# Hash attention and a gelu feed-forward on one core: the order of the first loads and hashes, and the mark that lets GpSimd's weight sums go

## The chip, the cores and the metric

The kernel runs on one core of a Trainium2 chip. A core has a matrix engine (TensorE, "PE" in the profile; "PEld" is its loading of weights), a vector engine (VectorE, DVE), a scalar engine (ScalarE, ACT), a general engine (GpSimd, POOL) and an engine that issues transfers (SyncE, SP). Transfers are carried out by 16 DMA engines; here they are issued from the queues of SP and ACT. The metric is the device time of one execution in microseconds. Before the change it is 857.73 us, the median of three runs from 857.51 to 859.04.

## The reference

The reference is an attention in which a query sees only the keys of its own hash bucket, followed by a feed-forward block. Cut to what matters:

```python
# q, k, v: (4, 8, 768, 64) f32; proj: (64, 6); w_in: (512, 2048); w_out: (2048, 512)
q_bits = (einsum('bhsd,dk->bhsk', q, proj) > 0)
k_bits = (einsum('bhsd,dk->bhsk', k, proj) > 0)
mask = bucket(q_bits)[:, :, :, None] == bucket(k_bits)[:, :, None, :]
scores = where(mask, q @ k.T / sqrt(64), -1e9)
attn = softmax(scores)
x = (attn @ v).transpose(0, 2, 1, 3).reshape(3072, 512)
h = x @ w_in
g = h / (1 + exp(-1.702 * h))
out = g @ w_out
```

## The kernel before

The attention takes two heads at a time: 16 pairs, each with 768 queries in two halves (c = 0, 1) of 384 columns, and 768 keys in six tiles of 128. For each tile of keys `scores` (line 426) puts four products into one PSUM tile: two of bf16 hash features (`kf`, `qf`), which push the entries of other buckets far down, and two of the f32 operands (`kT`, `qT`). ACT takes the exponential into `es`; POOL and DVE add up the denominators (`add_low`, `add_high`); `values` multiplies with v; `total`, `invert` and `norm` divide by the sums.

For pairs 1 to 15 k and q come in already in blocks that DVE turns (`turn`), and their hash bits are made two pairs ahead (`hashed`, `featured`; the features then go through small transfers on SP). The first pair has no such lead and goes through `first_pair` (line 345). It issues, each half on SP and ACT, the loads of k, of the projections `pj`, and of q, in this order. PE runs four matmuls on a tile of zeros (`idle`, cleared by DVE at line 76) that nobody reads; `hash_weights` (line 123) makes the hash weights `pf_k`, `pf_q` (and the wide `pf0`) on DVE from `pj` in ten small instructions. `turned` transposes one half of k or q with PE against the identity, and a copy takes it out of PSUM: DVE for both halves of k, ACT for both halves of q. `bits` multiplies a half with the hash weights and DVE makes the features from it (line 377). `measure` lets ACT square k or q and add up (the `junk` rows; a guard against sizes that are too large). The call order is k half 0, k half 1, q half 0, q half 1, then the hashes of k half 0, q half 0, k half 1; the hash of q half 1 is called `rest` and follows the first three score tiles. The PSUM tiles of this stage come from one pool of three banks (`sps`, tag "s"), which the score tiles use afterwards; another pool, `mps` (tag "m"), has one bank that the pair's later hashes and the second half of the values use.

While the attention runs, w_in is read in chunks of 512 KB (`raw`, line 161) and converted by DVE in small steps (`convert`), one chunk for each pair from pair 2 on; `begin(n)` (line 517) issues the load and `step` the work. `behind(x)` (line 316) is a helper that lets DVE clear a few words of a tile that a load will overwrite, so that the load has to wait for this place in DVE's order. It stands ahead of two loads of the attention, pair 1's v and pair 2's q (pairs are counted from 0).

The feed-forward block follows. Both of its products are done by a scheme with seven block products in place of eight, which needs sums of blocks of the operands. In the second product, h w_out, there are 21 such steps (three blocks of tokens times the seven outer products, in the order `OUTER` = 1, 2, 6, 7, 5, 3, 4), and each step is itself seven products of 128x256 (`product_of_halves`, line 1066), in the order 1, 2, 3, 6, 7, 5, 4. A step needs four sums of its right operand, made by DVE in the step before (`g_sums`: t1, t2, d12, t4; line 222 makes t1, 224 t2, 223 d12 and 225 t4). The fourth product reads t2, the fifth d12, the sixth t1, the seventh t4. It also needs four sums of its left operand, the weights (`inner_sums`), of which the third product reads the last; these are made once, for the first block of tokens, by POOL. A copy of one element by POOL, the `mark` (line 1234), stands ahead of POOL's sums in steps 2, 3, 5 and 6, and makes POOL wait for the tile that it reads: in step n, the first quarter of the result of step n-1, `ms[OUTER[n-1]]`, which DVE writes early in step n-1. So the sums stand in step n's part of the program, but POOL makes them for step n+1 while step n-1 or n runs. Steps are counted from 0; step 0 starts at 593.82 us, and each takes about 12.1 us.

Four engines (PE, DVE, ACT, POOL) execute the order that the program writes; SP's transfers are put in order by a scheduler that takes their waits into account. The conversion of w_out and a second path for large inputs are not touched.

Of the kernel before, what the change touches and what calls it, by code (L numbers as in the profile page):

```python
# [8 lines left out]
F32 = mybir.dt.float32  # L9
BF16 = mybir.dt.bfloat16  # L10
# [9 lines left out]
P = 128  # L20
# [18 lines left out]
def kernel(  # L39
# [17 lines left out]
    nc = tc.nc  # L57

    loader = [nc.sync]
    B, H, S, D = q.shape  # L60
    NB = proj.shape[1]
# [6 lines left out]
    HS = HT * P  # L68
# [3 lines left out]
    fixed.enter_context(tc.manual_schedule(engines=ORDERED))  # L72
    const = ctx.enter_context(tc.tile_pool(name="const", bufs=1))

    idle = const.tile([P, 512], BF16, name="idle")
    nc.vector.memset(idle, 0.0)
    ident = const.tile([P, P], F32, name="ident")
    make_identity(nc, ident)
    ones = const.tile([P, D], F32, name="ones")
    nc.vector.memset(ones, 1.0)  # L80

    later = []

    pj = const.tile([P, NB], F32, name="pj")

    def offsets(name, row):
        x = const.tile([P, 1], F32, name=name)
# [63 lines left out]
    for x in (0x3FFFFFFF, 0xFF800000):  # L153
        m = const.tile([P, 1], U32, name=f"mask_{x:x}")
        later.append((m, x))
        masks[x] = m.to_broadcast([P, CW])

    def convert(cv, dst, src, queue=None, psum=None):


        raw = cv.tile([P, CW, 2], U32, tag="raw", name="raw")
        (queue or loader[0]).dma_start(out=raw, in_=src)

        def of(x):
            return x if len(dst.shape) == 2 else x.rearrange("p (x r) -> p x r", r=dst.shape[2])

        lo, hi = raw[:, :, 0], raw[:, :, 1]
        bits = cv.tile([P, CW], U32, tag="bits", name="bits")
        if psum is None:
            part, size = dst.bitcast(U32), hi.bitcast(F32)  # L170
        else:
            part = psum.tile([P, CW], U32, tag="part", name="part")
            size = psum.tile([P, CW], F32, tag="size", name="size")
        yield


        if psum is None:
            nc.vector.scalar_tensor_tensor(part, hi, 3, masks[0x3FFFFFFF], op0=Alu.logical_shift_left, op1=Alu.bitwise_and)
        else:
            nc.vector.tensor_scalar(part, hi, 3, 0x3FFFFFFF, op0=Alu.logical_shift_left, op1=Alu.bitwise_and)  # L180
        yield
        nc.vector.scalar_tensor_tensor(bits, hi, 0xC0000000, part, op0=Alu.bitwise_and, op1=Alu.bitwise_or)
        yield

        if psum is None:
            nc.vector.tensor_tensor(part, bits, masks[0xFF800000], op=Alu.bitwise_and)
        else:
            nc.vector.tensor_scalar(part, bits, 0xFF800000, None, op0=Alu.bitwise_and)

        nc.scalar.activation(size, hi.bitcast(F32), Act.Square)  # L190
        part = part.bitcast(F32)
        yield
        nc.vector.scalar_tensor_tensor(part, lo, 2.0**-52, part, op0=Alu.mult, op1=Alu.mult)
        yield
        bits = bits.bitcast(F32)
        whole = bits if psum is not None else dst
        nc.vector.tensor_tensor(whole, bits if psum is not None else of(bits), part if psum is not None else of(part), op=Alu.add)
        yield

        nc.vector.scalar_tensor_tensor(dst, of(size), (1.125 * 2.0**-15) ** 2, of(whole) if psum is not None else whole,  # L200
                                       op0=Alu.is_ge, op1=Alu.mult)
# [3 lines left out]
    in_chunks = [(w_in_sb[:, kc, f : f + CW], wi[kc, :, f : f + CW])  # L205
                 for f0 in range(0, FF // 2, CW) for f in (f0, FF // 2 + f0) for kc in range(KC)]
# [79 lines left out]
    def attention(ff):  # L286
# [4 lines left out]
        with actx:  # L291
            ld = actx.enter_context(tc.tile_pool(name="ld", bufs=1))
            wk = actx.enter_context(tc.tile_pool(name="wk", bufs=2))
            cv = actx.enter_context(tc.tile_pool(name="cv", bufs=1))
            st = actx.enter_context(tc.tile_pool(name="st", bufs=2))
            aps = actx.enter_context(tc.tile_pool(name="aps", bufs=1, space=PSUM))
            mps = actx.enter_context(tc.tile_pool(name="mps", bufs=1, space=PSUM))
            early = actx.enter_context(ExitStack())
            ep = early.enter_context(tc.tile_pool(name="ep", bufs=1))
            sps = early.enter_context(tc.tile_pool(name="sps", bufs=GT, space=PSUM))  # L300
# [44 lines left out]
            def first_pair():  # L345


                b, hp = pairs[0]
                x = {}
                for i, (name, src) in enumerate((("k", k), ("q", q))):  # L350
                    raw = raws[0, name] = ld.tile([P, S // 32, 32], F32, tag=name, name=name)
                    x[name] = raw.rearrange("p s i -> p (s i)").rearrange("p (j t d) -> p j t d", j=2, d=D)
                    for j, queue in enumerate((nc.sync, nc.scalar)):
                        queue.dma_start(out=x[name][:, j], in_=src[b, 2 * hp + j].rearrange("(p t) d -> p t d", p=P))
                    if i == 0:
                        for j, queue in enumerate((nc.sync, nc.scalar)):
                            queue.dma_start(out=pj[D * j : D * (j + 1)], in_=proj)
                    xts[0, name] = wk.tile([P, S], F32, tag=f"{name}T", name=f"{name}T")

                nc.scalar.activation(const.tile([1, 1], F32, name="first"), ones[0:1, 0:1], Act.Exp)  # L360
                for _ in range(4):
                    nc.tensor.matmul(aps.tile([P, 512], F32, tag="av", name="warm"), idle[:, 0:P], idle, start=True, stop=True)
                hash_weights()

                def turned(name, c, move):
                    tp = sps.tile([P, 2, 512], F32, tag="s", name="tp")[:, 0, 0:HS]
                    for i in range(GT):
                        for j in range(2):
                            nc.tensor.matmul(tp[D * j : D * (j + 1), i * P : (i + 1) * P], x[name][:, j, c * GT + i, :], ident,
                                             start=True, stop=True)  # L370
                    move(xts[0, name][:, c * HS : (c + 1) * HS], tp)

                def bits(name, c):
                    cols = slice(c * HS, (c + 1) * HS)
                    h = sps.tile([P, 2, 512], F32, tag="s", name="hash0")[:, 0, 0:HS]
                    nc.tensor.matmul(h, pf0[name].rearrange("p j d -> p (j d)"), xts[0, name][:, cols], start=True, stop=True)  # L376
                    nc.vector.tensor_scalar(feats[0][name][:, cols], h, above0[name][:, 0:1], FEAT[name],
                                            op0=Alu.is_gt, op1=Alu.mult)

                measure(0, "k")  # L380
                turned("k", 0, nc.vector.tensor_copy)
                turned("k", 1, nc.vector.tensor_copy)
                turned("q", 0, nc.scalar.copy)
                turned("q", 1, nc.scalar.copy)
                measure(0, "q")
                bits("k", 0)
                bits("q", 0)
                bits("k", 1)
                return lambda: bits("q", 1)

# [121 lines left out]
            conv = {}  # L512
# [4 lines left out]

            def begin(n):
                if 0 <= n - 2 < len(in_chunks) - LATE:
                    conv[n] = convert(cv, *in_chunks[n - 2])  # L520
                    step(n)


# [40 lines left out]
            for n in range(1, last + 1):  # L564
# [44 lines left out]
                if n < last:  # L609
                    begin(n + 1)  # L610
# [87 lines left out]
    def feed_forward(tag, late=()):  # L698
# [8 lines left out]
        OUTER = (1, 2, 6, 7, 5, 3, 4)  # L707
        with ExitStack() as fctx:
# [324 lines left out]
            def g_quarters(n):  # L1033
                if n not in g_tiles:


                    g_tiles[n] = wholes[4:6] if n == 1 else [
                        (st2 if n % 2 else gp).tile([P, F4, TH], F32, tag=t, name=t + "ab"[n % 2]) for t in ("t1", "t2")]
                    g_tiles[n] = g_tiles[n] + [gp.tile([P, F4, TH], F32, tag="t4", name="t4g")]
                g = raw_g[n % 2]  # L1040
                x = [g[:, F4 * k : F4 * (k + 1), TH * j : TH * (j + 1)] for k in range(2) for j in range(2)]
                return x + g_tiles[n]
# [9 lines left out]
            def turned(c, i, j, q0, q1):  # L1052

                for q in range(q0, q1):
                    h, k = divmod(q, 2)
                    y = ys[j].rearrange("p b (d r) -> p r b d", r=4)[:, 2 * i + h, k * (TH // 32) : (k + 1) * (TH // 32), :]
                    nc.vector.transpose(y, c[:, q].rearrange("p (b t) -> p b t", t=32))  # L1057
# [79 lines left out]
            cv = cv_ctx.enter_context(tc.tile_pool(name=f"cv{tag}", bufs=1))  # L1137
# [31 lines left out]
            x = todo.pop(1, [])  # L1169
# [56 lines left out]
            ms, pending = {}, []  # L1226
            mark = st2.tile([1, 1], F32, name="mark")
            for n, (sb, o) in enumerate(steps_out):
# [2 lines left out]
                    fetch(n + 1)  # L1231

                if n in (2, 3, 5, 6):
                    nc.gpsimd.tensor_copy(mark, ms[OUTER[n - 1]][0:1, 0, 0:1])
                for f in {2: inner_sums(3), 3: inner_sums(4), 5: inner_sums(5) + inner_sums(6)[:2], 6: inner_sums(6)[2:]}.get(n, []):
                    f()
                later_sums = g_sums(n + 1)
                m = wholes[n % len(wholes)]
# [92 lines left out]
```

## Time and profile before

| what | value |
|---|---|
| median of three runs | 857.73 us (857.51 to 859.04) |
| the profiled execution | 858.67 us |
| its span on the core | 856.80 us |
| granted TensorE clock, mean | 0.998 |
| PE busy, 0 to 11 us | 9.23 us |
| PE busy, 11 to 600 us | 588.9 of 589 us |
| PE busy, 627 to 640 us | 12.75 of 13 us |
| PE busy, 840 to 856.8 us | 8.29 of 16.8 us |
| DVE busy, 600 to 627 us | 25.67 of 27 us |
| POOL busy, 600 to 627 us | 17.66 of 27 us |

Busy times are those of the profiled execution. The starts in the order of time are counted from the start of its span, and 1.87 us lie outside it. A row of the order of time may hold several instructions in a row (xN); its duration reaches from the start of the first to the end of the last. What stands in brackets at its end is the idle time of the engine just before it, and what ended it.

### The profile page before, as it was taken

The page shows a single profiled execution, that of the slowest core. Times are in us where ns is not written, and L with a number is a line of the kernel's source. Part 1 is how long each engine was busy: PE and PEld are TensorE (multiplying, and loading weights), DVE is VectorE, ACT ScalarE, POOL GpSimd, SP SyncE. Part 2 cuts the span into 40 slices and gives each one's busy share as a digit, 9 for nine tenths or more (in the row PEclk, how much of TensorE's full clock was granted, in tenths as well). Part 3 has the DMA queues.
Part 4 walks back from the last instruction along what each step waited for, and adds up shares of the span by engine and source line. Part 5 has one row for each costly group of instructions (what it writes and reads, how often), then busy time and mean ns, then how long its engine had stood idle before and what let it go on. Part 6 is the DMA issues. An engine that isn't in the chain of part 4 may idle for free.

```text
span 856.8 us, 13648 instructions
## 1 busy us (share of the span) xinstructions
PE 846.2 (99%) x5007; PEld 529.2 (62%) x5007; DVE 703.3 (82%) x1072; ACT 344.9 (40%) x549; POOL 353.4 (41%) x316
## 2 busy tenths in 40 slices
PE   9999999999999999999999999999999999999996
PEld 4444444444444444566666666545888888888885
DVE  4589999999999885788987788577998977797776
ACT  5866667777666654343444444433000000000000
POOL 4343333433433359996854476669725000000000
PEclk9999999999999999999999999999999999999999
DMA  5625755445563104436555546587745685467524
GB/s 131 101 47 107 113 89 85 85 86 99 115 97 71 47 26 150 144 134 233 194 204 217 221 153 234 202 278 257 275 151 190 192 254 197 155 191 245 197 99 101
DMA packets 160987, 132.11 MB, mean 154 GB/s; under 512 B 122608, under 2 KB 137616, under 8 KB 155536
## 3 DMA queue, kind: packets, MB, share of 16 engines
q1 hardware_dynamic: 152016, 106.63, 45.0%
q10 hardware_dynamic: 8896, 24.53, 8.3%
q8 instruction: 41, 0.67, 0.3%
q14 instruction: 34, 0.28, 0.1%
HBM read 79.69 MB, written 50.33 MB: 152 GB/s over the span
## 4 chain that ended last, share of the span: by engine, by line
PE 96%; DVE 2%; DMA 1%; ACT 0%; issue 0%; ACTq 0%; SPq 0%; DVEq 0%
PE product L1077 28%; PE product L751 22%; PE ps L435 18%; PE av L468 15%; PE small L819 6%; PE product L819 3%; PE dn L489 1%; PE hash L411 1%; DVE xT L1081 1%; DVE y L1057 1%; DMA pj<-in_proj_dram 1%; PE hash L376 0%; DVE v L1081 0%; DVE raw_g L223 0%; DVE t2a L224 0%
## 5 line engine op out<-in xcount | busy, mean ns | idle before, releaser
L436 ACT ACTIVATE e<-ps 128x768 f32<-128x768 f32 x192 | 151.2, 812 | 25.7 <-PE ps L435 23.1
L435 PE MATMUL ps<-qT,kT 64*128 64x384 f32 x768 | 155.1, 482 | 0.0
L443 POOL TENSOR_TENSOR acc<-e 128x768 f32<-128x768 f32 x32 | 51.8, 1617 | 193.8 <-ACT e L436 174.3
L468 PE MATMUL av<-e,v 128*32 128x385 f32 x1536 | 128.0, 487 | 0.0
L751 PE MATMUL product<-xT,w_in_sb 128*128 128x512 f32 x216 | 100.1, 593 | 0.1
L468 PEld LDWEIGHTS av<-e,v 128*32 128x32 f32 x1536 | 48.5, 109 | 76.2 <-issue 74.6
L435 PEld LDWEIGHTS ps<-qT,kT 64*128 64x128 f32 x768 | 68.0, 187 | 38.5 <-issue 38.4
L751 PE MATMUL product<-t_x,s_in 128*128 128x512 f32 x192 | 89.4, 592 | 0.0
L1090 ACT COPY u<-product 128x256 f32<-128x256 f32 x21 | 7.8, 372 | 172.2 <-PE product L1077 139.0
L751 PEld LDWEIGHTS product<-xT,w_in_sb 128*128 128x128 f32 x216 | 40.9, 190 | 36.5 <-issue 33.0
L435 PE MATMUL ps<-qf,kf 64*128 64x384 bf16 x384 | 62.9, 324 | 0.1
L444 POOL TENSOR_TENSOR acc<-acc,e 128x768 f32<-128x768 f32 x32 | 55.8, 1744 | 2.5
L751 PEld LDWEIGHTS product<-t_x,s_in 128*128 128x128 f32 x192 | 36.5, 190 | 29.7 <-issue 26.8
L449 DVE SCALAR_TENSOR_TENSOR acc<-e 128x768 f32<-128x768 f32 x32 | 47.7, 1490 | 5.1 <-ACT e L436 5.1
L767 DVE TENSOR_TENSOR u<-product,u 128x256 f32<-128x256 f32 (+1 forms) x60 | 28.4, 486 | 16.4 <-PE product L819 13.2
L435 PEld LDWEIGHTS <-kf 64*128 64x128 bf16 x384 | 18.9, 94 | 35.1 <-issue 6.2
L451 DVE TENSOR_TENSOR acc<-acc,e 128x768 f32<-128x768 f32 x32 | 34.3, 1072 | 3.3
L451 DVE TENSOR_TENSOR acc<-acc,acc 128x768 f32<-128x768 f32 x32 | 31.2, 974 | 6.3 <-POOL acc L444 3.2
L1077 PE MATMUL product<-raw_g,xT 128*128 128x256 f32 x152 | 35.1, 379 | 0.0
L222 POOL TENSOR_TENSOR u<-v,u 128x1024 f32<-128x1024 f32 (+1 forms) x11 | 23.9, 2168 | 21.9 <-ACT v L764 8.1
L767 DVE TENSOR_TENSOR v<-product,v 128x512 f32<-128x512 f32 x24 | 16.5, 689 | 19.4 <-PE product L751 19.4
L767 DVE TENSOR_TENSOR c<-small,c 128x256 f32<-128x256 f32 (+1 forms) x54 | 24.1, 460 | 8.8 <-PE small L819 8.6
(278 smaller groups left out, 1727.3 us busy)
## 6 DMA issues: line engine op xcount, KB each, us to landing
raw_g<-g_dram SPq DMA_DIRECT2D x22, 1024.0 KB
s_in<-g_dram SPq DMA_DIRECT2D x20, 1024.0 KB
g_dram<-c ACTq DMA_DIRECT2D x18, 512.0 KB
raw<-in_moe_w_out_dram ACTq DMA_DIRECT2D x16, 512.0 KB
raw<-in_moe_w_in_dram SPq DMA_DIRECT2D x15, 512.0 KB
v<-in_v_dram SPq DMA_DIRECT2D x32, 192.0 KB
k<-in_k_dram SPq DMA_DIRECT2D x60, 96.0 KB
q<-in_q_dram SPq DMA_DIRECT2D x60, 96.0 KB
```

The source lines that it names most:

```text
L222: return [lambda: eng.tensor_tensor(t1, b12, b11, op=Alu.subtract), lambda: eng.tensor_tensor(b12, b22, b12, op=Alu.subtract), lambda: eng ...
L435: nc.tensor.matmul(ps[:, j, 0:HS], a[hs, keys], m[hs, cols], start=not last, stop=last)
L436: nc.scalar.activation(es[c][:, kt, :, 0:HS], ps[:, :, 0:HS], Act.Exp, scale=1.0 / D**0.5)
L443: nc.gpsimd.tensor_tensor(acc, es[c][:, 0, :, 0:HS], es[c][:, 1, :, 0:HS], op=Alu.add)
L444: nc.gpsimd.tensor_tensor(acc, acc, es[c][:, 2, :, 0:HS], op=Alu.add)
L449: nc.vector.scalar_tensor_tensor(acc, e[0], T * TINY, e[1], op0=Alu.add, op1=Alu.add)
L451: nc.vector.tensor_tensor(acc, acc, x, op=Alu.add)
L468: nc.tensor.matmul(av[D * j + d : D * j + d + 32, :], vt[:, t, j, d : d + 32], es[c][:, t, j, :], start=(t == 0), stop=(t == T - 1))
L751: nc.tensor.matmul(ps, wq[LEFT[i]][:, kc, :], xq[RIGHT[i]][:, kc, :], start=(start and kc == 0), stop=(kc == K2 - 1), skip_group_check=not ...
L767: nc.vector.tensor_tensor(dst, x, y, op=Alu.add)
L819: nc.tensor.matmul(x, wq[LEFT[i]], xq[RIGHT[i]], start=start, stop=True, skip_group_check=True)
L1077: nc.tensor.matmul(ps, wq[LEFT[i]][:, c, :], gq[RIGHT[i]][:, c, :], start=(c == 0), stop=(c == F4 - 1))
```

## The change

In the first pair, the loads of `pj` go behind those of q on both queues. The tile of zeros and its memset go; the warm-up now reads a constant 1.0 that the program's setup has written before the kernel's own instructions, and there are five matmuls in place of four. The first half of k is copied out of PSUM by ACT in place of DVE. The transposes of the second half of q move behind the hashes of k half 0 and q half 0, and ahead of the hash of k half 1; the hashes of q take their PSUM tile from `mps`.

The first chunk of w_in is now loaded with `behind`: one column of its tile is cleared by DVE in `begin(2)`, at the end of pair 1. In SP's order, its load moves from the place behind the first pair's v to the place behind the feature transfers of pair 3.

In steps 2 and 3 of the second product the mark reads t2 of the same step (`g_quarters(n)[5]`), which DVE writes late in step n-1, in place of the result of step n-1. Steps 5 and 6 keep theirs.

```diff
-    idle = const.tile([P, 512], BF16, name="idle")
-    nc.vector.memset(idle, 0.0)
+    pj = const.tile([P, NB], F32, name="pj")
...
-    def convert(cv, dst, src, queue=None, psum=None):
+    def convert(cv, dst, src, queue=None, psum=None, behind=None):
         raw = cv.tile([P, CW, 2], U32, tag="raw", name="raw")
+        if behind is not None:
+            behind(raw[:, 0, 0:1])
         (queue or loader[0]).dma_start(out=raw, in_=src)
...
                     for j, queue in enumerate((nc.sync, nc.scalar)):
                         queue.dma_start(out=x[name][:, j], in_=src[b, 2 * hp + j].rearrange("(p t) d -> p t d", p=P))
-                    if i == 0:
-                        for j, queue in enumerate((nc.sync, nc.scalar)):
-                            queue.dma_start(out=pj[D * j : D * (j + 1)], in_=proj)
                     xts[0, name] = wk.tile([P, S], F32, tag=f"{name}T", name=f"{name}T")
+                for j, queue in enumerate((nc.sync, nc.scalar)):
+                    queue.dma_start(out=pj[D * j : D * (j + 1)], in_=proj)
...
-                for _ in range(4):
-                    nc.tensor.matmul(aps.tile([P, 512], F32, tag="av", name="warm"), idle[:, 0:P], idle, start=True, stop=True)
+                for _ in range(5):
+                    one = [nc.const_aps.tensor(1.0, [P, x], BF16) for x in (P, 512)]
+                    nc.tensor.matmul(aps.tile([P, 512], F32, tag="av", name="warm"), *one, start=True, stop=True)
...
-                    h = sps.tile([P, 2, 512], F32, tag="s", name="hash0")[:, 0, 0:HS]
+                    if name == "q":
+                        h = mps.tile([P, HS], F32, tag="m", name="hash0")
+                    else:
+                        h = sps.tile([P, 2, 512], F32, tag="s", name="hash0")[:, 0, 0:HS]
...
-                turned("k", 0, nc.vector.tensor_copy)
+                turned("k", 0, nc.scalar.copy)
                 turned("k", 1, nc.vector.tensor_copy)
                 turned("q", 0, nc.scalar.copy)
-                turned("q", 1, nc.scalar.copy)
                 measure(0, "q")
                 bits("k", 0)
                 bits("q", 0)
+                turned("q", 1, nc.scalar.copy)
                 bits("k", 1)
...
-                    conv[n] = convert(cv, *in_chunks[n - 2])
+                    conv[n] = convert(cv, *in_chunks[n - 2], behind=behind if n == 2 else None)
...
                 if n in (2, 3, 5, 6):
-                    nc.gpsimd.tensor_copy(mark, ms[OUTER[n - 1]][0:1, 0, 0:1])
+                    nc.gpsimd.tensor_copy(mark, (g_quarters(n)[5] if n < 4 else ms[OUTER[n - 1]])[0:1, 0, 0:1])
```

## The prediction, on record before the result was known

> **What bounds the kernel now.** I read the busy shares first, then the chain of waits, then the order of time in the two stretches that the change touches: the first 11 us, and the steps of the second product around 605 to 645 us.
>
> ```profile
> PE 846.2 (99%) x5007; PEld 529.2 (62%) x5007; DVE 703.3 (82%) x1072; ACT 344.9 (40%) x549; POOL 353.4 (41%) x316
> ...
> PE 96%; DVE 2%; DMA 1%; ACT 0%; issue 0%; ACTq 0%; SPq 0%; DVEq 0%
> ```
>
> TensorE (PE) is busy for 846.2 of 856.8 us and is 96% of the chain. An edit that takes no matmul away can win only the 10.6 us in which PE stands idle, and what slow or useless matmuls cost. By stretches, PE is idle 1.8 us before 11 us, 0.25 us between 627 and 640 us, and 8.5 us behind 840 us, where the last outputs go out and nothing is changed. So the places to look at are two.
>
> The start, in order of time (start, duration, engine, line, what):
>
> ```profile
> 1.19 2.52 PE L362 MATMUL warm<-idle 128*128 128x512 bf16 x4 [1.19 <-DVE idle L76]
> 3.81 2.90 PE L369 MATMUL tp<-ident,k 128*64 128x128 f32 x24
> 5.68 0.48 DVE L130 SCALAR_TENSOR_TENSOR pf_k<-pj,ones 64x6 f32<-64x6 f32 x4 [3.58 <-DMA pj<-in_proj_dram]
> 6.46 1.03 PE L369 MATMUL tp<-ident,q 128*64 128x128 f32 x12
> 7.05 1.01 DVE L371 COPY kT<-tp 128x384 f32<-128x384 f32 x2
> 7.66 0.88 PE L369 MATMUL tp<-ident,q 128*64 128x128 f32 x12 [0.17 <-DVE kT L371]
> 8.46 0.91 PE L376 MATMUL hash<-kT,pf_k 128*128 128x384 f32 x2
> 9.21 0.81 PE L376 MATMUL hash<-qT,pf_q 128*128 128x384 f32 x2
> 9.86 0.81 PE L376 MATMUL hash<-kT,pf_k 128*128 128x384 f32 x2
> 10.13 0.62 DVE L377 TENSOR_SCALAR qf<-hash,above_q 128x384 bf16<-128x384 f32 x1
> 10.80 0.34 PE L435 MATMUL ps<-qf,kf 64*128 64x384 bf16 x2
> ```
>
> The projections reach DVE at 5.68, DVE makes the hash weights until 7.13, and only then copies kT; the second half of q waits for the bank that this copy frees (7.66); the first scores wait for qf (10.13 + 0.62 = 10.75) and start at 10.80. From there to 635 us PE runs without a gap, so what the first scores win is kept. The k group's 24 rows take 2.90 us, 0.121 each, the last q group's 12 take 0.88, 0.073 each: PE is slow until about 6.5 us, although the page prints a full granted clock there.
>
> The steps of the second product:
>
> ```profile
> 613.59 0.17 POOL L1234 COPY mark<-xT 1x1 f32<-1x1 f32 x1 [1.94 <-DVE xT L1081]
> ...
> 615.20 1.41 DVE L1081 TENSOR_TENSOR v<-v,xT 128x256 f32<-128x256 f32 x1
> ...
> 616.53 2.90 DVE L1081 TENSOR_TENSOR xT<-xT 128x256 f32<-128x256 f32 x2
> ...
> 621.49 1.21 DVE L224 TENSOR_TENSOR t2a<-raw_g,t1a 128x1024 f32<-128x1024 f32 x1
> ...
> 634.35 1.22 DVE L224 TENSOR_TENSOR t2b<-s_in,t1b 128x1024 f32<-128x1024 f32 x1
> ...
> 635.67 1.97 PE L1077 MATMUL product<-t2b,w_in_sb 128*128 128x256 f32 x8 [0.25 <-issue]
> ```
>
> The mark lets POOL's four sums go at 613.7; while they run, the DVE additions of two SBUF tiles take 1.41 and 1.45 us against 0.43 in the quiet steps behind 640 us. This lag, and a second pass of POOL from 626.2 to 631.6, make t2b late: it ends at 635.57, while PE wants it one product (1.72 us) after 633.53, at 635.25. The step from 630.08 to 642.65 takes 12.57 us, the steps on both sides 12.09: the wait costs 0.48 us.
>
> **The change, part by part: the start.** DVE's memset of idle (0.27 us) goes, and the warm-up needs no engine: PE can start when the others do (ACT's and SP's first issues are at 0.73 and 0.74), about 0.75 in place of 1.19. Five matmuls at 0.64 (2.52 for four, with the gaps) end near 3.9; the array takes the next rows before the last one's end, and the k rows begin at 3.81 when k is there (ACT's first read of k starts at 3.87). Their cost is nothing under that wait; without it, at most 0.64.
>
> Queues: q moves up one place on SP and ACT (issue at about 1.2 in place of 1.8), pj falls one. The pj issue was at 1.20 and its data free at 5.68, 4.5 us later; from 1.8 to 2.0 that gives 6.3 to 6.5. Bounds: no earlier than k, 3.8; and as k, pj and q together were in by 6.46 in the old order, no later than about 6.5 if the DMA engines lose nothing by the swap. I take 6.4.
>
> PE, from starts: the k group holds it to 6.46. The first q group takes 1.0 (to 7.46). Hash k, 0.75 from start to next start, to 8.21; it needs pf_k, made 0.77 behind pj, 7.17, and the first kT half, now copied by ACT, which is free from 4.8 and needs 0.48. Hash q, 0.65, to 8.86; it needs ACT's copy of qT (7.53 + 0.48 = 8.01) and pf_q (pj + 1.45 = 7.85). The second q group, 0.80, to 9.66; its bank is free when DVE has copied the second kT half, pj + 1.45 + 0.55 = 8.40. The second hash k, 0.81, to 10.47. qf is ready at 8.21 + 0.81 + 0.11 + 0.62 = 9.75 and holds nobody. First scores at 10.47 in place of 10.80: **0.33 us**. The bank from the other pool is free: nothing has used it before.
>
> The clock: PE begins 0.44 us earlier, and if its rise comes as much earlier, slow rows (0.121 against 0.073) save 0.4 of that, **0.2 us**. Bounds: nothing, and 24 × 0.048 = 1.15 us if the whole k group runs fast. The nearest row is the one profiled rise, between 6.46 and 7.66, 5.3 us or more behind the first warm-up. I take 0.2. [...]
>
> The early load of raw (issued at 3.86) falls behind pair 3's feature transfers, which end on SP at 63.0, and behind a one-column DVE memset (0.06 by its like at 24.80). The next load of its kind goes out at 78.76 and its packets end at 82.0; so raw is in near 66.4, and DVE reads it at 67.37. The cover is 1.0 us. If it is late, what is late next on DVE is the features and the transpose of the denominators (72.26), which free a bank that PE asks for at 80.07: another 7 us. The loads queued behind it on SP slip 0.45 and are for pairs two rounds off. Cost: nothing; at most the lateness less 8 us.
>
> **POOL.** The mark now waits for t2 of the coming step. In step 1 DVE saves 1.41 − 0.43 and 2.90 − 0.88, 3.0 us: t2a ends near 619.7, not 622.70. POOL starts there and takes 5.4 (as 613.72 to 619.15) to 9.0 (four at the 2.25 of its rows at 599 to 609), so its sums are done by 625.1 to 628.7; PE needs them in the third product of step 3, 633.5. DVE's next sums now suffer, 1.21 to at most 2.28 (the row at 606.03): d12 of step 2 is done by 622.0 and wanted at 624.90, t4 by 624.7 and wanted at 628.35. In step 2 DVE saves 1.26 − 0.43 and 1.95 − 0.88, less up to 1.0 where POOL still runs: t2b ends near 633.7, 1.5 before PE asks. The wait goes: **0.48 us**. What is late next: d12 of step 3, 633.7 + 2.28 = 636.0 against 636.97, a cover of 1.0; and the sums for step 4, done by 642.7 at worst against 645.6. Bounds: 0 and 0.48.
>
> **Sum.** 0.33 + 0.2 + 0.48 = 1.0 us. The profiled execution took 858.67 (span 856.80 and 1.87 around it), so 857.7 by its own time; it lies 0.94 above the median, 857.73, and the forecast for the median is **856.7**.
>
> **Rivals.**
> 1. *The clock rises before the k group and pj is quick.* If PE's earlier start lets the rise come a whole step earlier, the chain ends at 10.47 − 1.1 = 9.4; pj must then be there by 5.7, as the scores cannot start before pj + 2.0 + 0.8 + 0.81 = pj + 3.6. Start 1.45, with POOL 1.9: 855.8. For it: pj was in at 5.68 once already, and PE starts 0.44 earlier. Against: only one rise was seen, late. [...]
> 2. *Only POOL's wait goes.* The start stays at 10.80, because a slow q or the extra change between transposes and hashes eats the 0.33: 857.25. For it: of the 1.8 us of idle PE before 11 us, 1.2 lie ahead of the warm-up, so only 0.6 lie in this chain, and its work stays.
> 3. *The projections come late (slower).* pj is now the last of three; each us beyond 6.7 costs a us of start, since hash k follows pj by 0.77. From 7.7 on it outweighs everything else; at 8.7 the scores start at 12.3, and with POOL's gain the time is 857.73 + 1.5 − 0.48 = 858.75. For it: this was the stage's longest wait (3.58), and from 4.6 to 6.8 us the DMA engines are 9 tenths busy. Against: 1.5 KB each, and the 6.46 bound. [...]
> 4. *POOL doesn't do what it says:* d12 or t4 of step 3 becomes the wait. Over 1.0 us of lag it costs PE the rest; 0.5 us lost makes 857.7.
>
> **How the numbers follow.** Forecast 0.46, rivals 0.20, 0.17, 0.10 and 0.07. The range that should hold 8 in 10 reaches from 855.5, a little below rival 1, to 858.2, short of rival 3. About 0.2% (1.7 us) is what a measurement of this kernel can tell from no change. Faster by that needs rival 1 or the best of the forecast: 0.23; slower needs a pj later than 9.4, or a loss that I don't see: 0.07; within: 0.70.
>
> **What would show it.** Right: the first scores at 10.2 to 10.5, no PE gap before t2b, the step at 630 in 12.09 us, POOL's marks near 620 and 634. Wrong: pf_k starting later than 6.7; k rows still slow to the end and scores at 10.8; a new PE wait for d12 near 637; a PE gap behind 67 us where raw is read.

## The result, and the profile after

The changed kernel takes 860.34 us (median of 21 runs, 858.62 to 861.22). The kernel before, run beside it, takes 858.64 us (21 runs, 857.51 to 859.49). The ratio is 1.0016, with a 95% interval from 1.0010 to 1.0022: slower by 0.9 to 1.9 us. 856.7 was forecast, with a range up to 858.2.

The page of the changed kernel shows hardly anything of it. PE's share and the chain of waits read as before:

```profile
PE 847.3 (99%) x5008; PEld 529.1 (62%) x5008; DVE 700.5 (82%) x1071; ACT 345.2 (40%) x550; POOL 357.8 (42%) x316
...
PE 96%; DVE 2%; ACT 0%; issue 0%; ACTq 0%; DVEq 0%
```

The span grew from 856.80 to 858.78 us. Where the 1.98 us arise is found by subtracting the start of each PE row before from the start of the same row after, and looking where the difference jumps:

| place | shift gained (-) or lost (+), us |
|---|---|
| first scores, 10.80 to 10.68 | -0.12 |
| denominators of pair 1, about 50 us | +0.56 |
| rows of lines 751 and 819 near 386 and 402 us | +0.18 |
| step at 630 us (POOL, t2b) | -0.51 |
| from the start of the last matmul to the end of the span, 8.89 to 10.76 | +1.87 |

The start, in order of time (start, duration, engine, line, what), PE's rows of the changed kernel:

```profile
0.77 3.15 PE L359 MATMUL warm<-const-bfloat16-1.0 128*128 128x512 bf16 x5 [0.77 <-PEq L1319]
3.93 2.91 PE L366 MATMUL tp<-ident,k 128*64 128x128 f32 x24
6.51 1.10 PE L366 MATMUL tp<-ident,q 128*64 128x128 f32 x12
7.54 0.91 PE L376 MATMUL hash<-kT,pf_k 128*128 128x384 f32 x2
8.29 0.81 PE L376 MATMUL hash<-qT,pf_q 128*128 128x384 f32 x2
9.03 0.88 PE L366 MATMUL tp<-ident,q 128*64 128x128 f32 x12
9.84 0.91 PE L376 MATMUL hash<-kT,pf_k 128*128 128x384 f32 x2
10.68 0.34 PE L435 MATMUL ps<-qf,kf 64*128 64x384 bf16 x2
```

The order is the foretold one, without a wait between the rows, but the k group still takes 2.91 us: the warm-up began 0.42 us earlier and the clock rose no earlier. The trace's clock record puts the rise at 6.82 us before and 6.95 us after.

The second product, POOL's marks, DVE's t2b and the PE rows that read it:

```profile
620.35 1.11 POOL L1235 COPY mark<-t2a 1x1 f32<-1x1 f32 x1 [8.11 <-DMA s_in<-g_dram]
...
632.52 1.11 POOL L1235 COPY mark<-t2b 1x1 f32<-1x1 f32 x1 [4.86 <-DVE t2b L221]
```

```profile
631.24 1.22 DVE L221 TENSOR_TENSOR t2b<-s_in,t1b 128x1024 f32<-128x1024 f32 x1
```

```profile
634.13 1.89 PE L1077 MATMUL product<-s_in,w_in_sb 128*128 128x256 f32 x8
635.86 1.89 PE L1077 MATMUL product<-t2b,w_in_sb 128*128 128x256 f32 x8
```

t2b ends at 632.46, 3.4 us before PE takes it up at 635.86, and no gap stands ahead of that row. The step runs from 630.67 to 642.76, 12.09 us as foretold (12.57 before).

The two losses lie elsewhere. DVE's sums of pair 1 before and after, then the PE rows that wait for them (`dn`, the denominators) and the next ones, before and after:

```profile
40.92 0.95 DVE L449 SCALAR_TENSOR_TENSOR acc<-e 128x768 f32<-128x768 f32 x1
41.97 0.96 DVE L451 TENSOR_TENSOR acc<-acc,e 128x768 f32<-128x768 f32 x1
```

```profile
40.94 0.94 DVE L449 SCALAR_TENSOR_TENSOR acc<-e 128x768 f32<-128x768 f32 x1
42.41 0.96 DVE L451 TENSOR_TENSOR acc<-acc,e 128x768 f32<-128x768 f32 x1 [0.53 <-ACT e L436]
```

```profile
50.34 0.94 PE L489 MATMUL dn<-acc,ones 128*32 128x384 f32 x8
51.22 0.34 PE L435 MATMUL ps<-qf,kf 64*128 64x384 bf16 x2
```

```profile
50.22 1.51 PE L489 MATMUL dn<-acc,ones 128*32 128x384 f32 x8
51.66 0.34 PE L435 MATMUL ps<-qf,kf 64*128 64x384 bf16 x2
```

The first sum starts alike, the second 0.44 us later, and so does everything behind it on DVE until the last sum, which PE awaits at 50.3 us with no margin: it ended at 50.39 before and at 50.83 after. With the 0.12 by which PE now asks earlier, PE loses 0.56. The view names ACT's exponential as the releaser, but that is not it: the count of ACT's results that this instruction waits for was reached at 36.34 us. Nothing that the profile shows holds DVE between 41.9 and 42.4.

At the end, SP's own waits behind 850 us (waited for: sum, times, longest, in us), before and after:

```profile
SPq L1294 <- SPq L1294: 2.0, 2, 1.0
```

```profile
SPq L1295 <- SPq L1295: 3.9, 2, 2.9
```

SP waits for the landing of the last outputs, 2.9 us in one piece instead of 1.0. Each of the last two transfers lands in 16 parts. Before, all 32 are in by 854.92. After, 15 of each 16 are in by 854.73, and the last ones come at 856.71 and 856.90, as if one DMA engine of the 16 were 2 us late (the records name no DMA engine). And the queue that brings instructions (q14: packets, MB, share of the 16 engines' time) in the window from 852.0 to 854.6, before and after:

```profile
q14 instruction: 2, 0.02, 1.9%
```

```profile
q14 instruction: 3, 0.02, 5.3%
```

5.3% of 16 engines for 2.6 us are 2.2 us of one engine, against 0.8 before. The trace's records of these 8 KB transfers, start in us and duration in ns:

```
before           848.73/309   853.06/309   853.97/478   855.52/399   856.47/307
after            853.00/885   853.88/885   854.10/440   857.19/474   857.48/361
```

After, the one at 848.73 is missing, and three stand close together while the last outputs go out.

### The profile page after: what moved, and what is told of

Same layout as the page of the kernel before. It is cut to its first block, busy times and chain, and to the rows that moved or that the text cites. A ratio compares the mean times of both kernels' runs of the same rounds, so it can differ in the third digit from the quotient of the medians.

```text
span 858.8 us, 13652 instructions
## 1 busy us (share of the span) xinstructions
PE 847.3 (99%) x5008; PEld 529.1 (62%) x5008; DVE 700.5 (82%) x1071; ACT 345.2 (40%) x550; POOL 357.8 (42%) x316
## 4 chain that ended last, share of the span: by engine, by line
PE 96%; DVE 2%; ACT 0%; issue 0%; ACTq 0%; DVEq 0%
PE product L1077 28%; PE product L751 22%; PE ps L435 18%; PE av L468 15%; PE small L819 6%; PE product L819 3%; PE dn L489 1%; PE hash L411 1%; DVE xT L1081 1%; PE tp L366 1%; DVE y L1057 1%; PE hash L376 0%; PE warm L359 0%; DVE v L1081 0%; DVE raw_g L220 0%
```

## Experiments

Two theories stood against each other. A: instructions reach an engine in blocks of 8 KB, and the change moved the borders of DVE's blocks. The records of the instruction queue q14 are of 8,192 bytes each (34 on the page, 0.28 MB). They name no engine, but one of its series of transfers comes when DVE has executed about 64, 192, 320, 448 instructions and so on, one for each 128 (before: at 40.79, 106.36, 171.50 and 239.00 us, with 63, 188, 318 and 447 begun). The change takes two DVE instructions away at the start (the memset of `idle`, a copy of kT), adds one (the memset ahead of raw) and saves one wait (at the new mark). DVE's 64th instruction on record was the first sum of pair 1 (line 449, behind an addition of 1.57 us); now it is the second (line 451), right behind a wait for the first. B: the new order of the loads, by which q of pair 2 is transposed at 35.60 in place of 34.58, and a chance of the output transfers.

Each run was timed beside the kernel before on the same chip. The table gives what their profiles show. "Places" is by how many instructions DVE's stream is longer (+) or shorter (-) than before, ahead of 50 us and at the end. "dn" is the time from the first row of pair 1's denominators to the next PE row. "End" is from the start of the last matmul to the end of the span (the expectations of e1, e2 and e4 speak of 10.6 and 12.5 us: the same end, counted from the last product's first weight load).

| kernel | places at 50 us, at the end | dn, us | end, us | ratio to before, 95% interval |
|---|---|---|---|---|
| before | 0, 0 | 0.87 | 8.89 | |
| after | -2, -2 | 1.44 | 10.76 | 1.0016 (1.0010 to 1.0022) |
| e1 after, 2 memsets at the start | 0, 0 | 0.87 | 8.90 | 0.9987 (0.9977 to 0.9996) |
| e2 before, DVE memsets to POOL | -2, -2 | 1.30 | 10.39 | 1.0020 (1.0011 to 1.0029) |
| e3 after, raw early | -2, -3 | 1.29 | 9.96 | 1.0014 (1.0005 to 1.0023) |
| e4 before, new mark | 0, -1 | 0.87 | 10.08 | 1.0011 (1.0002 to 1.0020) |
| e5 after, 2 memsets late | -2, 0 | 1.31 | 8.78 | 0.9993 (0.9984 to 1.0002) |
| e6 before, new mark, 1 memset | 0, 0 | 0.88 | 8.86 | 0.9989 (0.9980 to 0.9998) |
| e7 before, start changes, 2 memsets | 0, 0 | 0.87 | 8.91 | 0.9995 (0.9986 to 1.0004) |
| e8 e1 without warm-up | 0, 0 | 0.88 | 8.78 | 0.9997 (0.9988 to 1.0006) |
| e9 after, 1 memset at the start | -1, -1 | 0.89 | 10.06 | 1.0012 (1.0003 to 1.0021) |
| e10 e1 and 12 memsets late | 0, +12 | 0.89 | 8.82 | 0.9988 (0.9978 to 0.9998) |
| e11 e3, 3 memsets | 0, 0 | 0.88 | 8.66 | 0.9993 (0.9984 to 1.0002) |
| e12 e1 and 120 memsets late | 0, +120 | 0.87 | 8.79 | 0.9990 (0.9981 to 0.9999) |

### e1: the old places given back

```diff
+    pad = const.tile([1, 1], F32, name="pad")
+    for _ in range(2):
+        nc.vector.memset(pad, 0.0)
     ident = const.tile([P, P], F32, name="ident")
```

> The changed kernel with two DVE memsets of one word added at its start, which nobody reads; nothing else. Theory A (places in the instruction stream): DVE's 64th instruction is where a new block of instructions begins; the change took two DVE instructions away ahead of it, so that the block now begins behind a wait, and costs 0.45 us in the sums of pair 1, and at the end DVE's last block is read while the last outputs go out, which costs 1.9 us. The two memsets put every DVE instruction back to its old place: no late denominators at 50 us (next PE row 0.94 us as before, not 1.51), the last outputs in 10.6 us behind the last matmul's start, not 12.5, and about 857.9 us by a median of 858.64 for the kernel before (0.12 at the start and 0.5 from POOL are won). Theory B (the transfers: q of pair 2 comes 1 us later since the loads are in another order, and the long end is a matter of the output transfers themselves): nothing of it changes, 860.3 us.

858.13 us against 859.18 for the kernel before in the same session, and both losses gone:

```profile
40.95 0.94 DVE L452 SCALAR_TENSOR_TENSOR acc<-e 128x768 f32<-128x768 f32 x1
42.00 0.96 DVE L454 TENSOR_TENSOR acc<-acc,e 128x768 f32<-128x768 f32 x1
```

Two instructions that do nothing turn a kernel 0.16% slower into one 0.13% faster. Theory B, by which nothing should have changed, falls.

### e2: the losses without the change

```diff
-    nc.vector.memset(ones, 1.0)
+    nc.gpsimd.memset(ones, 1.0)
...
-            for f, eng in zip(feats, (nc.vector, nc.gpsimd)):
+            for f, eng in zip(feats, (nc.gpsimd, nc.gpsimd)):
```

> The kernel before, with three memsets (ones, and the first zeros of kf and qf) made by POOL in place of DVE, so that the instructions of DVE stand two places earlier; nothing else of the change. Theory A: the loss appears without the change: the denominators of pair 1 are 0.45 us late at 50 us, and if DVE's last block again falls between the last outputs, the end takes up to 1.9 us longer: 859.1 to 861.0 us against 858.6. Theory B: no loss, 858.6 us, and the end takes 10.6 us from the last matmul's start.

860.69 us against 859.18, denominators 0.43 us late, the end 1.50 us longer. Nothing of the change is in this kernel.

### e3 and e4: one part alone

e3 takes `behind` away from the first load of w_in; e4 puts only the new mark into the kernel before.

```diff
-                    conv[n] = convert(cv, *in_chunks[n - 2], behind=behind if n == 2 else None)
+                    conv[n] = convert(cv, *in_chunks[n - 2])
```

> The changed kernel with the load of the first chunk of w_in where it was before (no wait on DVE). Theory A: the place of DVE's instructions ahead of 50 us is that of the changed kernel, so the denominators stay 0.45 us late, though q of pair 2 may come earlier; at the end DVE stands one place earlier still, so the end is 10.6 or 12.5 us: 858.4 to 860.3 us. Theory B: the order of the loads returns to the old one, q of pair 2 is in 1 us earlier, and the 0.45 us at 50 us are back: 859.9 us or less.

860.17 us: the denominators stay late with the load in its old place, so its order is not the cause.

```diff
-                    nc.gpsimd.tensor_copy(mark, ms[OUTER[n - 1]][0:1, 0, 0:1])
+                    nc.gpsimd.tensor_copy(mark, (g_quarters(n)[5] if n < 4 else ms[OUTER[n - 1]])[0:1, 0, 0:1])
```

> The kernel before with the new mark alone (POOL waits for t2 in steps 2 and 3). Both theories: the step at 630 us in 12.09 us in place of 12.57, 0.5 us won, 858.1 us, with the start and the rows at 50 us as before. Theory A adds that one DVE wait fewer stands in the stream behind 630 us, so that the end may be 10.6 or 12.5 us: 858.1 or 860.0 us. Theory B: 858.1 us.

859.84 us against 859.18. PE starts its last matmul at 847.27 instead of 847.91, so POOL's wait is won, and the end gives back 1.2 us. SP's wait in e4:

```profile
SPq L1294 <- SPq L1294: 3.2, 2, 2.2
```

A part that works by itself measures as a loss, through one DVE wait that it saves.

### e5 and e6: the late places alone

In step 3 of the second product, two memsets for e5 (in the changed kernel), one for e6 (in e4's):

```diff
+                if n == 3:
+                    for _ in range(2):
+                        nc.vector.memset(pad, 0.0)
                 if n in (2, 3, 5, 6):
```

> The changed kernel with the two DVE memsets of one word put late, into step 3 of the second product (about 630 us), so that DVE's instructions stand in their old places at the end but not at 50 us. Theory A (places in the instruction stream, each loss by itself): the denominators of pair 1 stay 0.45 us late, the last outputs end about 8.9 us behind the last matmul (not 10.8), about 1.5 us faster than the changed kernel: 0.1 to 0.5 us above the kernel with both memsets at the start. Rival: the two losses hang together, or the memsets at the start helped in another way; then the end stays at 10 us or more and the time near 860.3 us by the shown median of the changed kernel.

> The kernel before with the new mark, and one DVE memset of one word in step 3 of the second product, in place of the one DVE wait that the new mark took away. Theory A: the end is as before, 8.9 us behind the last matmul (with the mark alone it was 10.1), and the 0.5 to 0.6 us of POOL's wait are won: ratio 0.9993 to the kernel before. Rival (the mark itself disturbs the end): 10 us again, ratio 1.001 as with the mark alone.

858.46 and 858.26 us against 858.98. In e5 the end is short and the denominators are late, so the two losses are separate. e6 differs from e4 by one memset of one word, and has an end of 8.86 us in place of 10.08, and a gain.

### e7 and e8: the start and the clock

e7 is the kernel before with all that the change does before 11 us and the two memsets of e1; e8 is e1 without the five warm-up matmuls:

```diff
-                for _ in range(5):
-                    one = [nc.const_aps.tensor(1.0, [P, x], BF16) for x in (P, 512)]
-                    nc.tensor.matmul(aps.tile([P, 512], F32, tag="av", name="warm"), *one, start=True, stop=True)
```

> The kernel before with the changes of the start alone (projections behind q, warm-up from the constant, the copies and transposes in the new order), raw and the mark as before, and two DVE memsets of one word at the start that keep DVE's places. The prediction's terms: 0.33 and 0.2 us won. Theory A now: the clock's rise falls between 6.2 and 8.8 us in the profiles so far, without regard to PE's first matmul; the shorter order wins at most 0.3 us, in a median 0 to 0.3: ratio 0.9997 to 1.0. Rival: the start in its new order is slower (first scores at 10.8 to 11.2 us in two profiles): ratio 1.0003 or more.

> The changed kernel with two DVE memsets at the start and without the five warm-up matmuls (they compute nothing that is read). If the clock rises a set time behind PE's first work (5.5 to 6.2 us behind it in the two profiles of before and after), it rises at 9.4 to 10.1 us, all transposes and hashes run slow, and the first scores come 1.0 to 1.5 us later. If the rise comes at its own time whatever PE does, the first scores stay at 10.7 to 11.2 us and the time is that of the kernel with the two memsets.

e7: 858.54 us against 858.98, first scores at 10.25 in its profile; the interval holds no change as well as a gain of 1.2 us. e8: 858.80 us, the clock rises at 10.00, later than in any other profile and 5.96 us behind PE's first work, and the first scores come at 12.19. So in this one profile the clock rose later where PE's first work came later (4.04 in place of 0.77), but over all profiles the distance is not a set time:

| profile | PE's first work, us | clock rises, us | first scores, us |
|---|---|---|---|
| old order: before, e4, e6, e2 | 1.19 | 6.82, 6.22, 8.75, 8.83 | 10.80, 10.74, 11.56, 11.58 |
| new order: e7, e5, after, e12, e1 | 0.77 | 5.98, 6.26, 6.95, 7.23, 7.29 | 10.25, 10.37, 10.68, 10.95, 10.84 |
| new order: e11, e9, e3, e10 | 0.77 | 7.50, 7.91, 8.24, 8.42 | 10.95, 11.27, 11.19, 11.37 |

By these profiles the rise comes 5.0 to 7.7 us behind the first work. Where it comes early, the new order wins 0.37 us (10.37 against 10.74 at 6.2); at 6.9 it is 0.12; where it comes late, next to nothing is left (11.37 with a rise at 8.42 against 11.56 at 8.75).

### e9: the border on the wait itself

The edit of e1 with one memset in place of two.

> The changed kernel with one DVE memset of one word at its start in place of two. The new block of DVE's instructions now begins with the wait behind the first sum (line 449), an instruction of 0.95 us, not with the sum behind that wait. Theory A, in its sharper form (the change of blocks costs about 0.45 us, and is hidden while a long instruction runs): the denominators at 50 us are in time (next PE row 0.87 us behind, not 1.3 to 1.44), while the end, one DVE place short as with the mark alone, takes 10.1 us or so and not 8.9: 1.2 us more than the kernel with two memsets, 859.3 us. Rival (only the exact old places are good): the denominators are late here too, and the time is 859.8 us.

```profile
41.38 0.95 DVE L452 SCALAR_TENSOR_TENSOR acc<-e 128x768 f32<-128x768 f32 x1
42.44 0.96 DVE L454 TENSOR_TENSOR acc<-acc,e 128x768 f32<-128x768 f32 x1
```

The second sum follows the first without the 0.5 us, although no instruction is in its old place, and the end takes 10.06 us: both as theory A had it. The time, 859.78 us against 858.79, is 0.5 above the expected one; the interval covers that, but it covers the rival's 859.8 as well, so it is the rows that decide.

### e10, e11, e12: other places, and raw

e10 and e12 put 12 and 120 memsets more into the second product of e1 (step 3; ten in each of the steps 7 to 18). e11 is e3 with two memsets at the start and one in step 3.

> The changed kernel with two DVE memsets at the start and twelve more in step 3 of the second product (about 0.06 us each, in DVE's slack). DVE's last block is then called for twelve instructions earlier. Theory A: some 4 us earlier than 848 us, ahead of the last outputs' crowd; the end stays at 8.8 to 8.9 us, and the time is that of the kernel with two memsets, ratio 0.9988 to the kernel before. Rival (the end is short only where DVE's instructions stand exactly in the old places): 10 us or more, ratio above 1.000.

> The changed kernel with the first load of w_in where it was before, two DVE memsets at the start and one in step 3 of the second product, so that every DVE instruction but those between 60 and 630 us has its old place. The prediction costed the later load at nothing: then this is the kernel with two memsets at the start, ratio 0.9988. If the later load costs or wins something, the two differ by more than 0.5 us; q of pair 2, 1 us later with the later load, is hidden by DVE's other work in both.

> The changed kernel with two DVE memsets of one word at the start and ten in each of the steps 7 to 18 of the second product (120; 0.11 us each, so 1.1 us a step, where DVE stands idle some 2 us of 12). DVE's blocks hold 128 instructions, so the places at the end are eight short of the old ones, more than in any of the slow ends so far (one to three short). Theory A: DVE now leaves for the program's end before it comes to the border of the block, no block is called for there, and the end is 8.9 us or less from the last matmul's start; about 858.2 us if the memsets delay no sum. Rival (every kernel with fewer instructions than the old places ends late): 10 us or more, 859.3 us.

e10: 858.03 us against 858.79, so old places are not needed, only harmless ones. That the block's transfer comes 4 us earlier was wrong: it stands at 848.71, where the better kernels have it. e11: 858.45 us against 858.79; against e1 and e10 no difference can be told, so no cost of the later load of raw shows (one of less than about 1 us would not). e12: 858.20 us against 858.83. DVE, eight places short of the border, leaves for the program's end before it, and one transfer less is on record:

```
e12              852.69/386   853.92/353   855.15/494   856.20/476
e4 (mark alone)  852.26/769   853.02/565   853.42/373   856.40/324   856.60/307
```

```profile
q14 instruction: 2, 0.02, 1.8%
```

This is e12's instruction queue between 852.0 and 854.6: back from 5.3% to 1.8%.

## Why the prediction was wrong, point by point

**The step that failed** is the first one, on where the time can change: the time behind 840 us "where the last outputs go out and nothing is changed" was taken as fixed, and the run up to 635 us as one in which "what the first scores win is kept". No edit touches either place, but the change shortens DVE's instruction stream, and both paid: 1.87 and 0.56 us, 2.4 together, against a forecast gain of 1.0. The prediction costed the removed memset and copy by their durations alone, and had no term for the place of what follows them. None of the four rivals had it either. With the places given back (e1) the change wins 1.05 us in the medians (859.18 to 858.13; the interval is 0.3 to 2.0), about the 1.0 forecast. That the two agree so closely is in part luck, as the clock's 0.2 in that sum is not shown by any run.

**POOL, 0.48:** right. 0.51 us in the profile; marks at 620.35 and 632.52 (about 620 and 634 foretold); t2b with a cover of 3.4 us (1.5 foretold), no wait for d12.

**Start, 0.33:** the mechanism was right, the size hangs on the clock. The rows came at 7.54, 8.29, 9.03, 9.84 and 10.68, each 0.1 to 0.2 later than worked out, and the projections were at DVE by 5.42, a microsecond earlier than the 6.4 assumed, so rival 3 fell. That also met rival 1's condition (5.7), but its early clock did not come: none of the nine profiles of the new order has a rise before 5.98. At equal clock (a rise at 6.2) the order wins 0.37. e7 measured 0.44 with an interval that includes nothing.

**Clock, 0.2:** not shown, either way. One rise had been seen, and it was taken as following PE's first work at a fixed distance. Between profiles with the same start the rise moves by 2.4 us (new order, 5.98 to 8.42) and 2.6 us (old order, 6.22 to 8.83); its mean is 7.3 us over nine profiles of the new order and 7.7 over four of the old, and with such a spread the difference says nothing. No run shows the fixed distance: the rise came 5.0 to 7.7 us behind the first work. Nor does any show the whole step by which rival 1 lets the rise come earlier.

**Raw, nothing:** right. DVE reads it at 67.81 without a wait, and e11 shows no difference.

**The two losses.** That they come from DVE's places in the instruction stream is shown: e1 removes both and e5 the second without undoing any part of the change, e2 makes them without it, and in all fourteen kernels the end is long at one to three places short and at no other offset tried. The extra tile `pad` is not the reason: e5 and e9 have it too, and each keeps one loss. The stop itself stands always at the same count: ahead of DVE's 64th instruction on record in the four kernels with late denominators, and ahead of the 1472nd in the five with a long end, which is 11 times 128 further on.

How the first arises is shown by e1, e5 and e9: DVE stops 0.43 us longer than usual at the border, and PE loses 0.42 to 0.57; it is seen when the border stands behind a wait, and not when a long instruction runs ahead of it. ACT has a like stop of 0.41 us at 38.84 in the changed kernel and at 39.00 in e1, ahead of its own 64th instruction, where nobody waits for it. Before, at the same count behind the addition of 1.57 us, DVE shows no stop.

How the second arises is argued: in the changed kernel DVE meets the border between its last instructions (a stop of 0.37 us more at 851.2, ahead of its last wait), its block is then brought at the same time as those that other engines ask for at the program's end, and these transfers (885 + 885 + 440 ns) would hold back the outputs of one DMA engine by 2 us. In the five kernels with a long end the last of 16 parts lands 1.4 to 2.4 us behind the fifteenth, in the nine others at most 0.5. In the five (after, e2, e3, e4, e9) three such blocks take 2.2, 2.1, 1.9, 1.7 and 1.6 us together, and the last part of the last outputs is 2.2, 1.9, 1.4, 1.4 and 1.5 us late. These times and e12 speak for it; the records don't name the DMA engine that a block or an output goes through.

**Open:** why e10's transfer stays at 848.71 though DVE meets the border twelve instructions earlier (a guess, not shown: it stands behind other transfers until these are through). The 0.18 us near 386 and 402 us are no effect of the change: e11 and e12 have such a shift and e1 has none, though e1 and e12 are the same program up to that place; they vary from execution to execution.

## What to carry to other kernels

Here two DVE instructions fewer moved the places of all that follow, and the 2.4 us that this cost outweighed the change's gain, 1.05 us in e1. In a kernel tuned to a fraction of a per cent, before a small part is judged, time it once more with the engine's instruction count restored by a memset that nobody reads. Look for borders right behind a wait on a path without margin (0.56 us here), and near the last outputs (1.87 us). e1 and e10 beat both kernels (0.9987 and 0.9988) by nothing else than the change and such memsets.

## What the runs showed of the hardware

The transfers of queue q14, 8 KB each, took 307 to 478 ns behind 848 us before the change and 361 to 885 ns after it. In the five kernels with a long end three of them, close together, took 1.6 to 2.2 us in all, and the last of an output's 16 parts landed 1.4 to 2.4 us behind the fifteenth. In the changed kernel DVE stopped 0.43 us longer than usual ahead of its 64th instruction on record and 0.37 ahead of its 1472nd, 11 times 128 further on, and ACT 0.41 us ahead of its own 64th; before the change, with an instruction of 1.57 us ahead of it, DVE's 64th came without a stop. TensorE's full clock lasted 846.505 us before as after. It rose between 5.98 and 8.42 us in nine profiles with the same start, and the first scores came between 10.25 (rise at 5.98) and 11.37 us (rise at 8.42).
